# Turning the spectrum back on VectorE instead of TensorE in a long-convolution kernel

## The chip, the cores and the metric

The kernel runs on one core of a Trainium2 chip. The metric is the device time of one execution in microseconds (us). The core has five engines with queues of their own: TensorE (PE in the profile, its weight loads PEld), VectorE (DVE), ScalarE (ACT), GpSimd (POOL) and SyncE (SP), which here only issues DMAs. Each engine takes its instructions in the order in which the program lists them, and waits for the others through semaphores.

## The reference

One batch of 2048 tokens with 512 channels, all in float32. Two branches read the same layer norm, and their product is added to the input:

```python
xn = layernorm(x)                                   # (1, 2048, 512)
# branch A: state space convolution
P  = exp(dt*(A_re + 1j*A_im)[:, :, None] * l)       # (512, 128, 2048)
K  = einsum("dn,dnl,dn->dl", Cc, P, dt*Bc).real     # one kernel of 2048 taps for each channel
y  = irfft(rfft(xn, 4096) * rfft(K, 4096))[:2048] + xn * Dskip
# branch B: feed forward, 512 -> 1792 -> 512
g  = silu(gelu(xn @ w1 + b1) @ w2 + b2)
return x + y * g
```

## The kernel before, in words

The kernel has two parts. In the first, up to about 406 us, the feed-forward matrix products run on PE, while the other engines make the convolution kernels K and store them in HBM (`kgd`), with the order of all work written out by hand in the string `ORDER`. The gate `g` goes to HBM as `gd`, one array of 128 rows for each block of 128 channels. The change leaves the order of this part alone; only the places of the tokens in the tiles that `ln_load` and `ln_store` read and write, and so in `gd`, are others.

The second part is the convolution. It is a transform of 2048 points in two steps (32 x 64) on the signal and on the kernel, a product, and the way back in two steps. It takes the channels in four blocks `b` of 128 (`NB`), and each block in eight slots `g`. `slot(b, g)` issues the work of one slot; a loop calls it for all 32, and some lines behind the loop finish the last block. Three blocks overlap in it: block `b` is in the middle, block `b + 1` gets its first transform, and block `b - 1` its way back. The steps, by the names that the profile shows:

- `first_dft` (line 864, PE, tile `s` from `in` and `fc`; called F here): 32 products into four PSUM banks; `first_out` (870, ACT) copies the four to `X`.
- `second_dft` (883, PE, tile `s` from `X` and `mc`; S): 32 products of 64x64 weights into a tile `ri` of two banks. `spectrum` (891, ACT) copies the signal's half to `uh`, `product` (900, DVE) multiplies twice into `t`.
- `combine` (910 and 912, DVE): after two slots it makes the real and imaginary parts `Y`, in four instructions on 64 partitions each.
- `back_dft` (918, PE, tile `sa` from `tcn` and `Y`; B): 8 products of 128x128 in two banks for one `Y`; `back_out` (930, ACT) copies them to `Z`.
- `swing` (936, PE, tile `w`): 32 transposes of 128x128 for a block, in eight groups of four; `swing_out` (944, ACT) copies them to `bs`.
- `last_dft` (975, PE, tile `y` from `bs` and `gc`; L) twice for a block; `last_out` multiplies by the gate on DVE (982) and adds the input on POOL (983); `store` (992) writes the output with eight DMAs from SP.
- `tail_load` (961, 964) brings the gate and the input for it: 24 DMAs from SP for a block; `side_load`, `side_turn`, `kernel_load` and `side_skip` bring the signal and the kernel of block `b + 2`, with two POOL copies (839).

[...] Two tiles `ri` take four. The other four are given out in turn by `bank`, two with the tag `c` and two with the tag `a`; F takes all four at once, B two, L two, a swing one. A tile is given again when its last reader is done. In the slot, S comes first on PE, then the rest; B stands in the odd slots, for the `Y` that was combined two slots before, and F in the even ones:

```python
sa = (b, i - 1) if i else (b - 1, 3)
if sa[0] < 0 or g % 2 == 0:
    sa = None
```

Of the kernel before, what the change touches and what calls it, by code (L numbers as in the profile page):

```python
# [20 lines left out]
P = 128  # L21
# [109 lines left out]
def _shape_constants():  # L131
# [4 lines left out]
    cg = np.zeros((2, N1, 2, 3, N1))  # L136
    for hh in range(2):
        for c, v in enumerate((np.cos(a).T, -np.sin(a).T)):
            cg[hh, :, c, 0] = v
            cg[hh, :, c, 1:].reshape(N1, N1, 2)[:, :, hh] = v  # L140
    cg = cg.reshape(P, 3 * N1)
# [14 lines left out]
    ct = ct.reshape(P, N1, 2, 2, 2, 16).transpose(0, 1, 4, 5, 3, 2)  # L156
# [16 lines left out]
def kernel(  # L173
# [7 lines left out]
    x_t = u[0].rearrange("(n h j t a q) d -> t h a j n q d", n=N1, h=2, j=2, t=2, a=2)  # L181
    o_l = out[0].rearrange("(r j q) d -> j r q d", j=2, q=NQ)
    o_t = out[0].rearrange("(n h j t a q) d -> t h a j n q d", n=N1, h=2, j=2, t=2, a=2)
    x_l = u[0].rearrange("(r j q) d -> j r q d", j=2, q=NQ)
# [3 lines left out]
    xs_l = xs.rearrange("(r j q) d -> j r q d", j=2, q=NQ)  # L188
# [125 lines left out]
    def ln_load(n):  # L314
        if n == 2:
            ln["zi"] = wka.tile([P, TB, D], F32, tag="zi", name="x23")
        if n in (2, 3):
            x = ln["zi"][:, 2 * n - 4:2 * n - 2, :]
        else:
            x = wka.tile([P, 2, D], F32, tag="x", name=f"x{n}", bufs=2)  # L320
        for j in range(2):
            SY.dma_start(x[j * 64:(j + 1) * 64], x_l[j, :, 2 * n:2 * n + 2, :])
        ln[n] = x
# [31 lines left out]
    def ln_store(n):  # L355
        for j in range(2):
            SY.dma_start(xs_l[j, :, 2 * n:2 * n + 2, :], ln[n][j * 64:(j + 1) * 64])
# [430 lines left out]
    def open_mid():  # L788
# [3 lines left out]
        SB["gc"] = pm.tile([P, N1], F32, name="gc")  # L792
# [109 lines left out]
    def combine(b, j, c, eng, js=slice(0, 4)):  # L902
        t, w = sm[b, j]
        if (b, j) not in yy:
            yy[b, j] = SB["pm"].tile([P, 4, 2, P], F32, tag="Y", name=f"Y_{b}_{j}", bufs=2)
        Y = yy[b, j].rearrange("p j a (r x) -> p a r j x", r=2)
        for ka in range(2):
            r = slice(ka * 64, ka * 64 + 64)
            if c == 0:
                eng.tensor_sub(Y[0:64, ka, :, js], t[r, 0, :, js], w[r, 1, :, js])  # L910
            else:
                eng.tensor_add(Y[64:128, ka, :, js], t[r, 1, :, js], w[r, 0, :, js])

    def back_dft(b, j, h):
        Y = yy[b, j].rearrange("p j a m -> p (j a) m")
        p = bank(f"sa{b}_{j}_{h}")
        for e in range(4):
            PE.matmul(p[:, e, :], Y[:, 4 * h + e, :], SB["tcn"][:, 8 * j + 4 * h + e, :], start=True, stop=True)  # L918
        yy[b, j, h] = p

    def back_out(b, j, h, engs=(A,)):
        if (b, "Z") not in yy:
            yy[b, "Z"] = SB["pm"].tile([P, 32, 2, N1, 2], F32, tag="Z", name=f"Z{b}", bufs=2)
        k = 8 * j + 4 * h
        src = yy.pop((b, j, h)).rearrange("p k (x h c) -> p x h k c", h=2, c=2)
        dst = yy[b, "Z"][:, :, :, k:k + 4, :]
        w = 4 // len(engs)
        for i, eng in enumerate(engs):
            n = slice(w * i, w * i + w)
            eng.copy(dst[:, :, :, n], src[:, :, :, n]) if eng is A else eng.tensor_copy(dst[:, :, :, n], src[:, :, :, n])  # L930

    def swing(b, q4, jj, wide=None):
        Z = yy[b, "Z"].rearrange("p (j r t q) h k c -> p j r t q (h k c)", j=2, r=2, t=2)
        p = bank(f"w{b}_{q4}_{jj}") if wide is None else wide[:, jj]
        for e in range(4):
            PE.transpose(p[:, e, :], Z[:, jj, q4 // 2, q4 % 2, e, :], ident)  # L936
        yy[b, q4, jj] = p

    def swing_out(b, q4, jj, eng):
        if jj == 0:  # L940
            yy[b, q4, "s"] = SB["pm"].tile([P, 2, 4, P], F32, tag="bs", name=f"bs{b}_{q4}", bufs=3)
        dst = yy[b, q4, "s"][:, jj].rearrange("p e (x r) -> p e r x", r=2)
        src = yy.pop((b, q4, jj)).rearrange("p e (r x) -> p e r x", r=2)
        A.copy(dst, src) if eng is A else V.tensor_copy(dst, src)

    gx = {}
    gc2 = dsk.rearrange("p b d -> p (b d)")[:, :2 * N1]

    def tail_load(b, i, q=SY, rows=False):
        cs = slice(b * P, (b + 1) * P)  # L950
        t = gx.pop((b, i, "t"), None) or new_tail(b, i)
        gx[b, i] = t
        if rows:
            n = slice(4 * i, 4 * i + 4)
            q.dma_start(t[0], gd[b].rearrange("p (q m) -> p q m", m=P)[:, n])
            for j in range(2):
                q.dma_start(t[1][j * 64:(j + 1) * 64], x_l[j, :, n, cs])
            return
        for a in range(2):
            r = slice(a * 64, (a + 1) * 64)  # L960
            q.dma_start(t[0][r], gd[b].rearrange("(j n h) (t a q m) -> t h a j n q m", n=N1, h=2, t=2, a=2, m=P)[i // 2, i % 2, a])
            for j in range(2):
# [212 lines left out]
```

## Time and profile before

| | us |
|---|---|
| median of the runs (3) | 560.42 |
| lowest and highest run | 559.8, 560.91 |
| span of the profiled execution, first to last instruction | 558.0 |
| PE, DVE, ACT, POOL busy in it | 540.2, 454.2, 407.8, 296.3 |
| the four blocks of slots and the end, in the span | 405.89 to 558.0 |

The profiled execution's own time outside the profiler is not listed; its span is 2.42 us under the median, and that difference stands for what lies around the span. A line of the timeline gives the start, the length to the modelled end of the last instruction, the engine, the line, the tiles and the count; PE's float32 products appear as two records each, so B is x16, F, S x64. On PE, the distance from one start to the next is what a group takes, since the ends overlap.

### The profile page before, as it was taken

Reading aid. Unit: us, or ns where it says so; the run is one execution under the profiler, and the core shown is the slowest. Engines: PE = TensorE matmul, PEld = TensorE weight load, DVE = VectorE, ACT = ScalarE, POOL = GpSimd, SP = SyncE. Lnnn points to the kernel's source line nnn. Section 1 sums busy time; section 2 is a strip of 40 time slices with the busy share of each in tenths; the row PEclk is TensorE's granted clock in tenths of the full one; section 3 lists DMA queues with packets and bytes.
Section 4 is the critical chain, followed back from the end, with each engine's and each line's share of the span. In section 5 each row is a group of like instructions: output and inputs, shape, how many; then the busy total and the mean of one; then the engine's idle time right before and its main releaser. Section 6 shows DMA issues by size and latency. Waiting matters only on the chain.

```text
span 558.0 us, 17143 instructions
## 1 busy us (share of the span) xinstructions
PE 540.2 (97%) x7179; PEld 432.1 (77%) x7179; DVE 454.2 (81%) x697; ACT 407.8 (73%) x602; POOL 296.3 (53%) x403
## 2 busy tenths in 40 slices
PE   8899999999999999999999999999999999999995
PEld 7567777777777777767777777777889998988872
DVE  6899999999997799988988969877357657767874
ACT  3589997977598999668989798995355565564542
POOL 5639585776966769857718747540320305014323
PEclk9999999999999999999999999999999999999999
DMA  8959337267468392426167049205965583615945
GB/s 188 288 161 311 84 96 210 61 210 228 135 189 269 133 295 81 143 75 192 57 188 219 21 114 186 61 11 181 365 245 79 140 128 95 191 46 127 197 120 113
DMA packets 108345, 86.92 MB, mean 156 GB/s; under 512 B 44294, under 2 KB 87562, under 8 KB 108268
## 3 DMA queue, kind: packets, MB, share of 16 engines
q1 hardware_dynamic: 97584, 65.37, 43.8%
q0 software_dynamic: 9568, 19.93, 12.1%
q8 instruction: 56, 0.92, 0.7%
q10 hardware_dynamic: 1116, 0.53, 0.4%
q14 instruction: 21, 0.17, 0.1%
HBM read 52.25 MB, written 33.55 MB: 154 GB/s over the span
## 4 chain that ended last, share of the span: by engine, by line
PE 68%; DVE 16%; issue 6%; DMA 5%; SPq 2%; ACT 1%; POOL 1%; DVEq 0%; POOLq 0%
PE z L295 8%; PE z L296 7%; PE z L297 7%; PE f L256 7%; PE f L258 7%; PE f L257 7%; PE s L883 6%; PE kg L656 5%; PE s L864 4%; PE sa L918 3%; DMA w2s<-in_B_w_dram 2%; PE ph L595 2%; PE w L936 2%; DVE e L641 2%; DVE hl L282 2%
## 5 line engine op out<-in xcount | busy, mean ns | idle before, releaser
L618 POOL TENSOR_TENSOR mm<-mm,rc 128x32 f32<-128x32 f32 (+4 forms) x150 | 110.7, 738 | 11.8
L295 PE MATMUL z<-w2h,hh 128*128 128x512 f32 x224 | 97.9, 437 | 0.0
L256 PE MATMUL f<-xh,w1h 128*128 128x512 f32 x220 | 92.0, 418 | 0.5 <-ACT hf L270 0.5
L297 PE MATMUL z<-w2h,hl 128*128 128x512 f32 x224 | 88.5, 395 | 0.9 <-DVE hl L282 0.9
L296 PE MATMUL z<-w2l,hh 128*128 128x512 f32 x224 | 88.7, 396 | 0.0
L258 PE MATMUL f<-xh,w1l 128*128 128x512 f32 x220 | 86.9, 395 | 1.5 <-DVE w1l L241 1.5
L257 PE MATMUL f<-xl,w1h 128*128 128x512 f32 x220 | 86.7, 394 | 0.0
L883 PE MATMUL s<-X,mc 64*64 64x128 f32 x2048 | 63.5, 272 | 0.9 <-issue 0.9
L900 DVE TENSOR_TENSOR t<-s,uh 128x512 f32<-128x512 f32 x64 | 41.1, 685 | 25.9 <-ACT uh L891 25.6
L883 PEld LDWEIGHTS s<-X,mc 64*64 64x64 f32 x2048 | 56.0, 133 | 4.8 <-issue 2.7
L641 DVE TENSOR_TENSOR e<-mm,ra 128x1024 f32<-128x1024 f32 x32 | 47.8, 1495 | 4.7 <-POOL mm L618 3.2
L297 PEld LDWEIGHTS z<-w2h,hl 128*128 128x128 f32 x224 | 42.1, 188 | 11.7 <-DVE hl L282 1.8
L258 PEld LDWEIGHTS f<-xh,w1l 128*128 128x128 f32 x220 | 41.3, 188 | 11.9 <-DVE w1l L241 2.1
L615 POOL COPY mm<-rc 128x32 f32<-128x32 f32 x30 | 15.4, 512 | 65.4 <-DVE e L648 49.0
L256 PEld LDWEIGHTS f<-xh,w1h 128*128 128x128 f32 x220 | 41.5, 189 | 10.3 <-ACT hf L270 1.2
L282 DVE TENSOR_TENSOR hl<-hf,hh 128x512 fp32r<-128x512 f32 x56 | 46.7, 838 | 3.4 <-ACT hh L276 3.3
L295 PEld LDWEIGHTS z<-w2h,hh 128*128 128x128 f32 x224 | 42.5, 190 | 9.0
L609 DVE SCALAR_TENSOR_TENSOR ra<-ra,ph 128x512 f32<-128x512 f32 x64 | 43.6, 681 | 6.9 <-ACT ra L603 6.0
L296 PEld LDWEIGHTS z<-w2l,hh 128*128 128x128 f32 x224 | 42.3, 189 | 7.9
L257 PEld LDWEIGHTS f<-xl,w1h 128*128 128x128 f32 x220 | 41.4, 188 | 8.9
L870 ACT COPY X<-s 128x512 f32<-128x512 f32 x56 | 28.9, 598 | 25.6 <-PE s L864 25.6
L645 DVE TENSOR_TENSOR e<-mm,ra 128x1024 f32<-128x1024 f32 x32 | 45.6, 1425 | 0.0
(185 smaller groups left out, 1146.2 us busy)
## 6 DMA issues: line engine op xcount, KB each, us to landing
x<-in_A_u_dram SPq DMA_DIRECT2D x16, 256.0 KB
xs<-x SPq DMA_DIRECT2D x16, 256.0 KB
xt_h<-xh POOLq DMA_DIRECT2D x4, 1024.0 KB, 5.4
xt_l<-xl POOLq DMA_DIRECT2D x4, 1024.0 KB, 7.3
kgd<-ko SPq DMA_DIRECT2D x32, 128.0 KB
za<-zo SPq DMA_DIRECT2D x4, 1024.0 KB
xh<-xt_h POOLq DMA_DIRECT2D x4, 1024.0 KB, 6.8
xl<-xt_l POOLq DMA_DIRECT2D x4, 1024.0 KB, 10.1
```

Of the source, the lines that this page charges most:

```text
L256: PE.matmul(p, wh[:, k, :], xh[:, k, :], start=(k == 0), stop=False)
L257: PE.matmul(p, wh[:, k, :], xl[:, k, :], start=False, stop=False)
L258: PE.matmul(p, wl[:, k, :], xh[:, k, :], start=False, stop=(k == KD - 1))
L282: V.tensor_sub(hl, hf, hh)
L295: PE.matmul(z, hh[:, s], wh, start=(f0 == 0 and not rows), stop=False)
L296: PE.matmul(z, hh[:, s], wl, start=False, stop=False)
L297: PE.matmul(z, hl[:, s], wh, start=False, stop=(f0 == FA - 1))
L609: V.scalar_tensor_tensor(ra[:, 0, c], ra[:, 1, c], MAGIC, p, op0=ALU.subtract, op1=ALU.subtract)
L618: GP.tensor_mul(mv[:, :, 0:3:2, w:2 * w], mv[:, :, 0:3:2, 0:w], rc[:, 2 + 2 * i:4 + 2 * i, :].rearrange("p j c -> p c j").unsqueeze(3).to_ ...
L641: V.tensor_mul(e1, m1.unsqueeze(1).to_broadcast([P, 2, CH, N1]), ra[:, :, :, :N1])
L645: V.tensor_mul(e2[:, :, :, :H], m2[:, :, :H].unsqueeze(1).to_broadcast([P, 2, CH, H]), ra[:, :, :, dn])
L883: PE.matmul(p[ka * 64:(ka + 1) * 64, r, o, :, jj], mc[h, k, ((0, 2), (1, 0))[c][o], :], xf[b][h, c, :, k, :], start=(c == 0), stop=(c == 1 ...
```

## The change

The way back is laid out anew.

- The tables `ct`, `cg` and the choice of `k` in `second_dft` are ordered so that the two halves of 64 partitions of the products belong to different frequencies. `combine` works on 128 partitions: two instructions for one `Y` in place of four.
- `back_dft` sums over real and imaginary parts in PSUM: 16 products of 64x128 weights, two row halves side by side, each half into a bank of its own. It moves from the odd slots to the even ones: for the `Y` that the slot before combined.
- The transposes on PE, their copies and `bs` go. `turn` transposes `Z` on DVE in squares of 32x32: four instructions of 128x1024 for a block, in slots 5 and 6 of the block and in slots 1 and 2 of the next.
- `last_dft` is one step for a block, in slot 3: 32 products of 32x32 weights on 512 columns, into four banks. `last_gate` multiplies by the gate with four DVE instructions with a stride of two; `store` adds on POOL in slots 4 to 7, with four DMAs each.
- `first_dft` of the next block stands in slots 0, 1, 5 and 6, no more in 0, 2, 4 and 6, and behind `back_dft` where a slot has both.
- `tail_load` is five DMAs for a block (the gate in one of 1 MB), in slots 0 and 1; gate and input have one buffer each (`gb`, `xb`), for a whole block. For the last block they come on POOL's queue in slot 1.
- Tokens: position (n, c, q), of 32, 4 and 16, where there was (r, j, q), in `ln_load`, `ln_store` and all that follows.

```diff
-                            k, h = 4 * g + 2 * jj + ka, slice(r * 64, (r + 1) * 64)
+                            k, h = 8 * (g // 2) + 4 * ka + 2 * (g % 2) + jj, slice(r * 64, (r + 1) * 64)
...
+            yy[b, j] = SB["pm"].tile([P, 2, 4, P], F32, tag="Y", name=f"Y_{b}_{j}", bufs=2)
+        Y = yy[b, j][:, c].rearrange("p j (r x) -> p r j x", r=2)
+        if c == 0:
+            eng.tensor_sub(Y[:, :, js], t[:, 0, :, js], w[:, 1, :, js])
+        else:
+            eng.tensor_add(Y[:, :, js], t[:, 1, :, js], w[:, 0, :, js])
+
+    def back_dft(b, j, wide=None):
+        Y = yy.pop((b, j))
+        ps = [bank(f"sa{b}_{j}_{a}") for a in range(2)] if wide is None else [wide[:, a] for a in range(2)]
         for e in range(4):
+            for c in range(2):
+                for a in range(2):
+                    r = slice(64 * a, 64 * a + 64)
+                    PE.matmul(ps[a][:, e, :], Y[r, c, e, :], SB["tcn"][r, 8 * j + 2 * e + c, :],
+                              start=(c == 0), stop=(c == 1), skip_group_check=True)
+        yy[b, j, "p"] = ps
+
+    def back_out(b, j, engs=(A, A)):
+        if j % 2 == 0:
+            yy[b, "Z", j // 2] = SB["pm"].tile([P, N2, 2, N1 // 2], F32, tag="Z", name=f"Z{b}_{j // 2}", bufs=2)
+        for a, p in enumerate(yy.pop((b, j, "p"))):
+            k = 8 * (j % 2) + 4 * a
+            dst = yy[b, "Z", j // 2][:, :, :, k:k + 4]
+            src = p.rearrange("p k (c n) -> p n c k", c=2)
+            A.copy(dst, src) if engs[a] is A else engs[a].tensor_copy(dst, src)
+
+    def turn(b, h, i, n=2):
+        if i == 0:
+            yy[b, "T", h] = SB["pm"].tile([P, N2, N1], F32, tag="T", name=f"T{b}_{h}", bufs=2)
+        m = slice(i * N2 // n, (i + 1) * N2 // n)
+        V.transpose(yy[b, "T", h][:, m].rearrange("p n c -> p (n c)"), yy[b, "Z", h][:, m].rearrange("p n c k -> p (n c k)"))
...
+    def last_dft(b, hs=(0, 1), gs=range(G)):
+        if (b, "y") not in gx:
+            gx[b, "y"] = [bank(f"y{b}_{q}").rearrange("p e m -> p (e m)") for q in range(G)]
+        py = gx[b, "y"]
+        for h in hs:
+            T = yy[b, "T", h]
+            for g in gs:
+                for q in range(G):
+                    r = slice(q * N1, (q + 1) * N1)
+                    PE.matmul(py[q][g * N1:(g + 1) * N1], SB["gc"][r, h], T[r, 16 * g:16 * g + 16].rearrange("p n c -> p (n c)"),
+                              start=(h == 0), stop=(h == 1), skip_group_check=True)
...
+    ahead = {0: (0, 0), 1: (0, 1), 5: (1, 0), 6: (1, 1)}
 
     def slot(b, g):
...
+        if sa[0] < 0 or g % 2:
             sa = None
+        u = None if last else ahead.get(g)
         second_dft(b, g)
         if sa:
+            back_dft(*sa)
+        if u:
+            first_dft(b + 1, *u, range(G))
+        if b and g == 3:
+            last_dft(b - 1)
         spectrum(b, g)
         if sa:
+            back_out(*sa)
+        if u:
+            first_out(b + 1, *u)
         product(b, g)
+        if g % 2:
+            combine(b, i, 0, V)
             combine(b, i, 1, V)
+        if b and g in (1, 2):
+            turn(b - 1, 1, g - 1)
+        if g in (5, 6):
+            turn(b, 0, g - 5)
+        if b and g == 3:
+            last_gate(b - 1)
+        if b and 3 < g:
+            store(b - 1, g - 4)
...
+        wide = SB["ps"].tile([P, 2, 4, P], F32, tag="ri", name="wide", bufs=2)
+        back_dft(b, 3, wide)
+        last_dft(b, (0,))
+        back_out(b, 3, (A, V))
+        for i in range(2):
+            turn(b, 1, i)
+            last_dft(b, (1,), range(2 * i, 2 * i + 2))
+        last_gate(b)
+        for i, (eng, q) in enumerate(((V, SY), (V, A), (GP, SY), (GP, A))):
+            store(b, i, eng, q)
```

More of the change, by code (lines that the diff above doesn't have):

```diff
@@ L921, in back_out @@
[L921 to L944, printed above, removed]
+            yy[b, j] = SB["pm"].tile([P, 2, 4, P], F32, tag="Y", name=f"Y_{b}_{j}", bufs=2)
@@ L946, with tail_load @@
     gx = {}
[L947 to L949 removed]
+    def tail_load(b, q=SY, part=2, t=None):
         cs = slice(b * P, (b + 1) * P)
[L951 to L962, printed above, removed]
[L963 to L964 removed]
@@ L1029, in slot @@
         second_dft(b, g)
-        if b:
-            for q4 in ls.get(g, ()):
-                last_dft(b - 1, q4)
-                if not last:
-                    last_out(b - 1, q4, (GP, GP))
-                    store(b - 1, q4)
-        if nxt and g % 2 == 0:
-            first_dft(b + 1, i // 2, i % 2, range(G))
-        if sa:
-            back_dft(*sa, 0)
-            back_dft(*sa, 1)
+        if sa:
+            back_dft(*sa)
+        if u:
+            first_dft(b + 1, *u, range(G))
```

173 lines of the change are left out of this document (37 added, 136 removed).

## The prediction

> **What bounds the kernel now.** I read the page first, then the busy time of each engine in stretches cut where a block's first S starts, then the timelines of PE, ACT and DVE in the second block. The page's first line, and the stretches for blocks 0, 1, 2, 3 (up to the end of the last combine) and the end; columns are PE, PEld, DVE, ACT, POOL busy, PE's granted clock, the DMA share and GB/s.
>
> ```profile
> span 558.0 us, 17143 instructions
> ...
> 405.89:436.54 30.65, 29.80 (x817) 27.47 (x816) 19.31 (x30) 16.96 (x31) 7.10 (x8) 1.00 0.51 130
> 436.54:473.13 36.59, 36.59 (x897) 32.70 (x896) 23.55 (x36) 21.66 (x40) 7.92 (x8) 1.00 0.67 133
> 473.13:509.63 36.50, 36.50 (x898) 32.60 (x897) 24.76 (x36) 21.65 (x40) 5.91 (x7) 1.00 0.44 119
> 509.63:541.83 32.20, 30.43 (x651) 26.41 (x650) 28.03 (x45) 14.91 (x26) 14.19 (x22) 1.00 0.74 166
> 541.83:558.00 16.17, 9.21 (x68) 5.49 (x66) 7.30 (x11) 3.87 (x7) 5.03 (x4) 0.93 0.45 99
> ```
>
> Blocks 1 and 2 are PE alone: it is busy all of 36.59 and 36.50 us, with DVE at 24 and ACT at 22. Whatever leaves PE there is gained, as long as PE then waits for nothing. So the question is not only what PE has to do, but how long before each step its inputs and banks are ready. PE's timeline gives the price of each step, from one start to the next:
>
> ```profile
> 453.87 1.98 PE L883 MATMUL s<-X,mc 64*64 64x128 f32 x64
> 455.78 2.01 PE L864 MATMUL s<-fc,in 32*128 32x64 f32 x64
> 457.72 1.98 PE L883 MATMUL s<-X,mc 64*64 64x128 f32 x64
> 459.63 1.09 PE L975 MATMUL y<-bs,gc 64*32 64x512 f32 x16
> 460.65 2.05 PE L918 MATMUL sa<-tcn,Y 128*128 128x128 f32 x16
> 462.54 1.91 PE L936 MATMUL w<-ident,Z 128*128 128x128 f32 x16
> 464.38 1.98 PE L883 MATMUL s<-X,mc 64*64 64x128 f32 x64
> ...
> 478.89 2.05 PE L918 MATMUL sa<-tcn,Y 128*128 128x128 f32 x16
> 480.88 1.98 PE L883 MATMUL s<-X,mc 64*64 64x128 f32 x64
> ```
>
> S takes 1.91, F 1.94, half of L 1.02, B 1.89 to 1.99 (I take 1.98), sixteen transposes 1.84. A block has eight S, four F, four B, two halves of L and 32 transposes: 15.28 + 7.76 + 7.92 + 2.04 + 3.68 = 36.68, the stretch of 36.5 to 36.6. The chains beside it, on ACT and on DVE:
>
> ```profile
> 455.96 0.59 ACT L891 COPY uh<-s 128x512 f32<-128x512 f32 x1 [1.03 <-issue]
> 457.81 2.05 ACT L870 COPY X<-s 128x512 f32<-128x512 f32 x4 [1.26 <-PE s L864]
> ...
> 462.74 0.59 ACT L930 COPY Z<-sa 128x512 f32<-128x512 f32 x1 [0.31 <-PE sa L918]
> ```
>
> ```profile
> 452.25 1.39 DVE L912 TENSOR_TENSOR Y<-t,t 64x512 f32<-64x512 f32 x2
> 453.65 1.40 DVE L910 TENSOR_TENSOR Y<-t,t 64x512 f32<-64x512 f32 x2
> 456.58 1.29 DVE L900 TENSOR_TENSOR t<-s,uh 128x512 f32<-128x512 f32 x2 [1.53 <-ACT uh L891]
> 460.81 1.35 DVE L982 TENSOR_TENSOR gb<-y,gb 128x512 f32<-128x512 f32 x2 [2.94 <-PE y L975]
> ```
>
> From the end of S (455.78) to its `uh` 0.18, from the end of F (457.72) to `X` 0.09, from B (462.54) to `Z` 0.20, from `uh` to the product 0.03. A copy takes 0.59 alone, 0.51 in a row of four; a product pair 1.29, a combine instruction 0.70, a gate instruction 0.68. And PE waits in order:
>
> ```profile
> 509.63 3.72 PE L883 MATMUL s<-X,mc 64*64 64x128 f32 x128
> 514.17 0.46 PE L918 MATMUL sa<-tcn,Y 128*128 128x128 f32 x2 [0.82 <-DVE Y L910]
> ```
>
> ```profile
> 511.12 2.21 DVE L912 TENSOR_TENSOR Y<-t,t 64x512 f32<-64x512 f32 x2
> 513.34 1.40 DVE L910 TENSOR_TENSOR Y<-t,t 64x512 f32<-64x512 f32 x2
> ```
>
> This is the one place where B came close to its `Y`: PE stood still, and went on 0.14 after the first of the two L910 (513.34 + 0.69). From any DVE or ACT release I count 0.10 to 0.14.
>
> **The change, part by part.** *Removed from PE:* the transposes, 3.68 in each of blocks 1, 2 and 3 and in the end. *L:* twice the 16 records of a half in a grid twice as fine; 2.04 if sixteen small tiles run at twice the rate of eight, 4.1 if not. Up to some 3 us it only shortens a wait below, so it costs nothing; at 4.1 about 1 us a block. *B:* as many column passes as before, two at a time; S, with the same passes in four small tiles, takes 1.91, so 1.98 stays, and 1.91 is the lower end. *Removed from ACT:* eight copies to `bs`; ACT was not the bound. *DVE:* combine halves, 16 times 0.70 becomes 8 times, 5.6 less; four turns are added. The trace has no DVE transpose. The nearest rows are a two-input DVE operation of the same 128x1024 at its fastest (from the chain), and a POOL copy of 128x1024 (from the groups):
>
> ```profile
> 206.52 1.13 DVE e L645
> ```
>
> ```profile
> L839 POOL COPY in<-raw 128x1024 f32<-128x1024 f32 x4 | 7.9, 1996 | 26.6 <-PE s L864 22.1 <-issue 4.4
> ```
>
> I take 1.13, the engine's own row; 2.00 is the upper end. At 1.13 DVE's block stays near 23 us. [...]
>
> *What is late next.* Four new waits come from the order in the slot.
>
> (1) B for a `Y` of the slot before. From the end of that slot's S: 0.18 + 0.59 + 0.03 + 1.29 + 0.03 + 1.40 + 0.12 = 3.64 until PE may read both halves of `Y`. If PE has only the next S in between (1.91), it waits 1.73; four of B's 32 records need only the first half, so 1.48. F or L in the odd slot covers it. Uncovered are slot 4 of block 0, slots 2 and 6 of block 3 (no F there), and slot 0 after every block.
>
> (2) F right behind B, in slots 0 and 6. F needs four banks with its first four products, B holds two: 0.20 + 0.51 + 0.59 + 0.10 = 1.40 of standing until both `Z` copies are out. Before, an S lay between.
>
> (3) F of slot 1 behind F of slot 0, and the first S of a block behind F of slot 6: the four `X` copies take 0.09 + 2.05 + 0.10 = 2.24, and one S of 1.91 lies between: 0.33.
>
> (4) L takes all four banks, and B of slot 4 needs two of them. The gates stand on DVE behind product and combine of slot 3: from the end of that S 0.18 + 0.59 + 0.03 + 1.29 + 0.03 + 1.40 + 2 x 0.68 + 0.12 = 5.00, less L and S of 3.95: 1.05.
>
> In a block's slot 0, (3) has held S by 0.33 while `uh` before it comes 0.1 later behind the copies, so (1) is 1.25 there.
>
> *The sum.* Block 0: no transposes to lose; slot 1 0.33, slot 4 1.48, slot 6 1.40: +3.2. Blocks 1 and 2: -3.68, and 0.33 + 1.25 + 1.40 in slot 0, 0.33 in slot 1, 1.05 in slot 4, 1.40 in slot 6, together 5.76: +2.1 each. Block 3 has no F: eight S, four B, L are 25.24; 0.33 + 1.25, 1.48, 1.05, 1.48 of waits are 5.59; then 3.52 from the last S to the last `Y`: 34.35 against 32.20, +2.15. POOL's four adds now follow the gates, and in the row at 511.12 combine beside POOL's adds took 2.21 for 1.39; once where nothing covers it: +0.8.
>
> The end, old rows first:
>
> ```profile
> 540.96 0.87 DVE L910 TENSOR_TENSOR Y<-t,t 64x256 f32<-64x256 f32 x2
> ...
> 545.74 1.29 DVE L944 COPY bs<-w 128x512 f32<-128x512 f32 x2 [0.74 <-PE w L936]
> ```
>
> ```profile
> 548.93 2.51 POOL L983 TENSOR_TENSOR last<-last 128x512 f32<-128x512 f32 x2 [1.92 <-DVE last L982]
> ```
>
> ```profile
> 550.23 2.76 SPq L992 DMA_DIRECT2D out_dram<-last  x6
> ```
>
> ```profile
> 551.47 0.88 ACTq L992 DMA_DIRECT2D out_dram<-last  x2
> 552.46 2.13 ACTq L1014 DMA_DIRECT2D out_dram<-last  x3
> ```
>
> The last `Y` was complete at 541.83, the last issue over at 554.59, and 3.4 later the span ends. New, from the last `Y`: B 1.85 after it, the copy on DVE 0.20 + 0.65, two turns 1.13 + 1.13, the last quarter of L 0.51 + 0.12: 5.6; four gates, since each store needs all four: 8.5. DVE's adds 9.2 and 9.9, POOL's (1.26 each) 9.8 and 11.0; four issues of 0.46 for each store, two stores on each queue: SP until 12.9, ACT until 13.5; with 3.4, 16.9 against 16.17: +0.7.
>
> *Costed at nothing.* Loads in the new token order have the same bytes in pieces of the same length, and the first part has no other work. SP issues 19 DMAs a block fewer; but the gate's 1 MB waits for the add of slot 7, which on POOL stands behind the two copies of `side_turn` (2.00 each), and behind it on SP stand the input's loads. The gate is first read in slot 3, some 20 us into the block, the input in slot 4: that slack hides it; without it each microsecond late counts. Behind SP's waits stand `side_load` and `kernel_load`, needed a block later.
>
> Together 3.2 + 2.1 + 2.1 + 2.15 + 0.8 + 0.7 = 11.05: a span of 569.1. The median of the runs is 2.4 above the span, so 571.5.
>
> **The rivals.** *Faster: PE passes its waits.* If PE's queue brings the next ready step forward (the S behind a waiting B, the B behind a waiting F), only the work counts: block 0 as before, blocks 1 and 2 -3.7 each, block 3 28.8 for 32.2, the end +0.7: 550 at best, 552 if DVE holds some of it. It decides where the waits of a middle block sum to less than 3.7. Against it: at 514.17 the rows are in program order and PE idles. *No change: the banks are free.* Without (2), (3) and (4), as if copies and gates came out in time, 1.40 x 5, 0.33 x 6 and 1.05 x 3 go, while (1) grows by 0.23 three times: 11.4 less, 560.1. Against: B's and L's tiles end whole, not one by one. *Smaller: `Y` is in time.* Without (1), three times 1.25 and 1.48, 8.2 less: 563.3. Against: the 3.64 is five rows in series. *Larger: weights show.* B's weight loads, from the groups:
>
> ```profile
> L918 PEld LDWEIGHTS sa<-tcn,Y 128*128 128x128 f32 x256 | 30.0, 191 | 8.3 <-issue 3.4 <-ACT uh L891 3.4 <-PE s L883 1.0
> ```
>
> If those of 64-row tiles were not hidden, 32 of 0.191 with two tiles at once make B 3.06, and fifteen of them add 16: 587. F, with weights as wide and 64 records in 1.94, speaks against.
>
> *Larger: the clock.* In the end stretch PE is busy 9.21 of 16.17 and was granted 0.93; in blocks at 95% and more, 1.00. With 5.8 of 38.8 idle PE would be busy 85% in a middle block. The end stretch lost 0.07 of 16.17 by the clock, 1.1; if each of the 14 waits over a microsecond lost as much, 15 would be added: 587. [...] The longest idle here is 1.5, and nothing in the trace of before shows it for waits that short.
>
> **How the numbers follow.** The forecast 0.68, with 562 to 578 for it: down to less overlap of waits and B at 1.91, up to turns at 2.00 (+3.2, mostly in block 3 and the end) and L at 4.1 (+3). Passing 0.09, banks free 0.05, `Y` in time 0.07, weights 0.06, clock 0.05. The range 560 to 582 leaves out passing, weights and clock, 0.20. A change under 0.2% could not be told here. Faster 0.09, the same 0.03 (half of the bank case), slower 0.88.
>
> **What would show it.** No `w` and `bs` rows; Y twice in place of four times. PE idle of about 1.5 ahead of `sa` in slot 4 of block 0, released by DVE `Y`; of 1.4 ahead of F in slots 0 and 6, released by ACT `Z`; of 1.0 ahead of `sa` in slot 4, released by the gates. Blocks of about 34, 38.7, 38.7 and 35. Wrong, if PE's busy share in blocks 1 and 2 is near all again, or if `turn` is over 2 us.

## The result, and the profile after

The changed kernel takes 700.19 us (median of 4 runs, 697.2 to 703.35) against 560.61 us (559.8 to 560.91) for the kernel before in the same runs: a ratio of 1.2493, 95% interval 1.2454 to 1.2531. Slower was forecast, but at 571.5 us. The profiled execution has a span of 701.6 us, 143.6 over the 558.0 before.

The page's first lines, and the slices of PE, its granted clock and the DMA rate:

```profile
span 701.6 us, 17483 instructions
...
PE 557.4 (79%) x7439; PEld 443.5 (63%) x7439; DVE 443.4 (63%) x675; ACT 390.8 (56%) x571; POOL 287.8 (41%) x390
...
PE   5242519389298959999999999999998979899772
```

PE is busy 557 us, much as before (540), in a span 144 us longer: the work hardly grew, the waiting did, and it stands at the left end, in the first part, which the prediction had set aside (the first S starts at 522.37, before at 405.89). The first 100 us, the kernel before ahead (columns as in the prediction):

```profile
0.00:100.00 100.00, 93.66 (x677) 73.50 (x678) 88.70 (x188) 76.50 (x119) 63.42 (x114) 1.00 0.68 187
```

```profile
0.00:100.00 100.00, 34.55 (x146) 28.19 (x146) 26.38 (x72) 14.84 (x25) 13.60 (x48) 0.68 0.24 77
```

PE does little more than a third of its work there, at a granted clock of 0.68, and the DMA engines move 77 GB/s for 187: an idle PE beside idle DMA engines. The loads come through SP's queue. Its timeline before, then after (start, us of issue, engine, line):

```profile
0.75 2.48 SPq L322 DMA_DIRECT2D x<-in_A_u_dram  x4
3.28 0.59 SPq L222 DMA_DIRECT2D w1s<-in_B_w_dram  x1
3.91 0.50 SPq L227 DMA_DIRECT2D w2s<-in_B_w_dram  x1
...
15.19 3.02 SPq L357 DMA_DIRECT2D xs<-x  x4
```

```profile
0.75 5.55 SPq L316 DMA_DIRECT2D x<-in_A_u_dram  x4
6.34 4.97 SPq L216 DMA_DIRECT2D w1s<-in_B_w_dram  x1
11.35 5.49 SPq L221 DMA_DIRECT2D w2s<-in_B_w_dram  x1
...
40.82 15.62 SPq L351 DMA_DIRECT2D xs<-x  x4
```

The same four loads and four stores of 256 KB, but the issue of one weight load behind them now takes 4.97 and 5.49 us where it took 0.59 and 0.50, and a stage that was stored at 15.19 is stored at 40.82. The rate, in 40 slices of the first 25 us (before, 111 to 439 from the fourth slice on):

```profile
GB/s 0 0 2 14 7 20 46 39 43 46 46 49 52 52 52 52 52 52 52 107 318 60 46 52 52 52 52 46 151 308 35 45 47 46 52 52 52 52 52 48
```

The plateau at 52 GB/s is the thing to see: it is not noise from a crowded path but a fixed rate. The diff has one change that could set it: `ln_load` and `ln_store` moved from 64 rows in one outer dimension to `x_l[2 * j:2 * j + 2, :, ...]`, an outer dimension of 2 over 32 rows each, on the DRAM side.

### The profile page after: what moved, and what is told of

It is laid out like the page before. It is cut to its first block, busy times and chain, and to the rows that moved or that the text cites. A ratio compares the mean times of both kernels' runs of the same rounds, so it can differ in the third digit from the quotient of the medians.

```text
span 701.6 us, 17483 instructions
## 1 busy us (share of the span) xinstructions
PE 557.4 (79%) x7439; PEld 443.5 (63%) x7439; DVE 443.4 (63%) x675; ACT 390.8 (56%) x571; POOL 287.8 (41%) x390
## 4 chain that ended last, share of the span: by engine, by line
PE 50%; DMA 17%; DVE 12%; SPq 9%; issue 6%; ACT 3%; POOL 2%; POOLq 0%; DVEq 0%; ACTq 0%
DMA lh<-pcd 8%; PE s L877 6%; PE f L250 5%; PE z L289 5%; PE f L251 5%; PE f L252 5%; PE z L290 5%; PE z L291 5%; DMA w2s<-in_B_w_dram 4%; PE sa L913 4%; PE kg L650 4%; PE s L858 3%; SPq L216 3%; DMA in<-kgd 3%; SPq L351 2%
## 5 line engine op out<-in xcount | busy, mean ns | idle before, releaser
L250 PE MATMUL f<-xh,w1h 128*128 128x512 f32 x220 | 95.1, 432 | 31.6 <-ACT hf L264 16.2
L612 POOL TENSOR_TENSOR mm<-mm,rc 128x32 f32<-128x32 f32 (+4 forms) x150 | 114.5, 763 | 11.9
L251 PE MATMUL f<-xl,w1h 128*128 128x512 f32 x220 | 89.5, 407 | 0.0
L252 PE MATMUL f<-xh,w1l 128*128 128x512 f32 x220 | 89.3, 406 | 0.0
L877 PE MATMUL s<-X,mc 64*64 64x128 f32 x2048 | 68.3, 282 | 10.3 <-issue 7.6
L877 PEld LDWEIGHTS s<-X,mc 64*64 64x64 f32 x2048 | 59.8, 139 | 17.2 <-issue 11.6
L609 POOL COPY mm<-rc 128x32 f32<-128x32 f32 x30 | 13.1, 435 | 111.5 <-DMA rc<-recd 59.5
L589 PE MATMUL ph<-cbs,lh 96*128 96x512 bf16 x64 | 25.6, 400 | 40.1 <-DMA lh<-pcd 36.0
L635 DVE TENSOR_TENSOR e<-mm,ra 128x1024 f32<-128x1024 f32 x32 | 45.9, 1433 | 9.4 <-POOL mm L612 6.4
L264 ACT ACTIVATE hf<-f,b1s 128x512 f32<-128x512 f32 x56 | 38.5, 689 | 15.6 <-PE f L252 10.5
```

What stands on the lines that cost most here:

```text
L250: PE.matmul(p, wh[:, k, :], xh[:, k, :], start=(k == 0), stop=False)
L251: PE.matmul(p, wh[:, k, :], xl[:, k, :], start=False, stop=False)
L252: PE.matmul(p, wl[:, k, :], xh[:, k, :], start=False, stop=(k == KD - 1))
L612: GP.tensor_mul(mv[:, :, 0:3:2, w:2 * w], mv[:, :, 0:3:2, 0:w], rc[:, 2 + 2 * i:4 + 2 * i, :].rearrange("p j c -> p c j").unsqueeze(3).to_ ...
L635: V.tensor_mul(e1, m1.unsqueeze(1).to_broadcast([P, 2, CH, N1]), ra[:, :, :, :N1])
L877: PE.matmul(p[ka * 64:(ka + 1) * 64, r, o, :, jj], mc[h, k, ((0, 2), (1, 0))[c][o], :], xf[b][h, c, :, k, :], start=(c == 0), stop=(c == 1 ...
```

## The experiments

Theory A: a DMA is shared out over as many DMA engines as its outermost dimension allows, so these loads and stores run on two of sixteen, and everything behind them on SP's queue waits. Theory B: the second part's new order lost the time and the first part only shows a late start. By A the outer dimension alone decides. A time with a ratio to the kernel before in brackets is the median of four runs; the others are of one run, beside 560.3 for the kernel before. All edits but the second are to the changed kernel, and from the fourth on its loads and stores of the layer norm are four DMAs.

**Four DMAs of 32 rows.**

```
-        for j in range(2):
-            SY.dma_start(x[j * 64:(j + 1) * 64], x_l[2 * j:2 * j + 2, :, 2 * n:2 * n + 2, :])
+        for c in range(G):
+            SY.dma_start(x[c * N1:(c + 1) * N1], x_l[c, :, 2 * n:2 * n + 2, :])
```

and the same in `ln_store`.

> The changed kernel, with the loads and stores of the layer norm in four DMAs of 32 rows each in place of two of 2 x 32 rows; the same bytes to the same places. Theory A (a DMA is shared out over the DMA engines by its outermost dimension, and that is 2 in the changed kernel): the first S of block 0 stands at 406 to 410 us again, as before the change (405.9), in place of 522.4; the second part still takes 175 to 180 in place of 152; about 585 to 590 in all. Rival B (the new places of the tokens in HBM are slow to read and write in any shape): the first part stays at about 520 and the whole at about 700.

586.13 us (1.0475, 1.0446 to 1.0504). **The kernel before, with the new order's loads alone** (`x_n` is its input seen as `(n c q) d -> c n q d`; the same in `ln_store`, nothing else):

```
-            SY.dma_start(x[j * 64:(j + 1) * 64], x_l[j, :, 2 * n:2 * n + 2, :])
+            SY.dma_start(x[j * 64:(j + 1) * 64], x_n[2 * j:2 * j + 2, :, 2 * n:2 * n + 2, :])
```

> The kernel before, with only the layer norm's loads and stores in the new token order and in two DMAs of 2 x 32 rows each; the way back is the old one, so gate and convolution meet at wrong tokens. If these transfers alone make the first part slow (theory A or rival B): the first S at 515 to 525 us, 670 to 680 in all. If the first part's loss comes from something else in the change (tables, placement in SBUF): 406 and about 561.

673.2 us, against 560.27. **One DMA with an outer dimension of 4**:

```
-        for j in range(2):
-            SY.dma_start(x[j * 64:(j + 1) * 64], x_l[2 * j:2 * j + 2, :, 2 * n:2 * n + 2, :])
+        SY.dma_start(x, x_l[:, :, 2 * n:2 * n + 2, :])
```

> The changed kernel, with each load and store of the layer norm in one DMA of 4 x 32 rows: fewer DMAs, outermost dimension 4. Theory A: twice as many DMA engines as with 2, so these transfers run at about twice the rate (near 100 GB/s where 50 is seen in the first 60 us), and half or more of the 116 us goes: first S at 440 to 470, 620 to 650 in all. Rival B: no better than the changed kernel, 522 and 700. If instead the count of DMAs mattered, half as many would bring some of it back without a change of the rate.

621.16 us. The rates of the three in the first 25 us, in the order told:

```profile
GB/s 0 0 42 263 269 256 223 262 210 207 211 307 280 33 169 241 356 254 216 202 232 256 282 236 243 203 223 252 331 420 348 203 151 216 169 215 291 316 365 317
```

```profile
GB/s 0 0 2 14 26 13 52 43 39 33 29 39 46 46 46 46 52 52 52 57 180 267 33 52 52 52 46 52 102 206 197 44 44 46 52 52 52 46 52 52
```

```profile
GB/s 0 0 3 26 0 13 46 217 266 84 92 95 164 324 57 83 81 79 105 105 105 105 105 105 88 79 80 31 110 320 280 257 195 162 141 37 26 52 111 262
```

Outermost 2: 52 GB/s, in either kernel. Outermost 4: 105. Outermost 32: no plateau, mostly 200 to 400. So 26 GB/s for each unit of that dimension where it is 2 or 4, and A holds for them. The places of the tokens in HBM are the same in all three, so they are not what is slow: the form of these 16 loads and 16 stores is worth 701.6 - 582.5 = 119 us of the 143.6, and costs the kernel before 113 when it is put in alone. The share of the 16 DMA engines agrees: on the plateau of the changed kernel (7.50 to 11.20) it is 0.13, where two of sixteen are 0.125; at 4 the slices at 105 GB/s show two tenths, where four of sixteen are 0.25; with 32 rows most slices show eight or nine tenths. Which engines carry a DMA is not shown.

**What is left.** With four DMAs the first S starts at 406.17, as before (405.89), and the second part takes 176.3 us for 152.1, +24.2 where the prediction had +11.05. Its stretches for blocks 1 and 3 and the end, cut as in the prediction:

```profile
440.25:485.25 45.00, 39.48 (x964) 34.20 (x960) 22.31 (x32) 17.16 (x33) 8.10 (x8) 0.92 0.56 113
...
524.60:562.90 38.30, 29.15 (x744) 24.43 (x736) 24.86 (x36) 9.61 (x18) 8.14 (x9) 0.98 0.62 136
562.90:582.50 19.60, 6.78 (x95) 3.20 (x92) 8.00 (x10) 0.58 (x1) 3.43 (x2) 0.69 0.25 54
```

Block 0 (34.08, forecast 33.85) and block 2 (39.35, 38.6) are near the forecast; block 1 (45.00, 38.7), block 3 (38.30, 35.15) and the end (19.60, 16.9) are not. PE's waits in these 176 us, by what ended them (total, times, longest):

```profile
PE s L877 <- issue: 6.9, 3, 3.8
PE sa L913 <- DVE Y L902: 5.3, 4, 2.0
PE wide L913 <- DVE Y L902: 2.9, 1, 2.9
PE y L954 <- issue: 1.5, 1, 1.5
PE s L858 <- ACT Z L924: 1.5, 5, 0.3
```

The lines with DVE and ACT are the forecast waits. The "issue" ones, waits that nothing in this view ended, are not: PE stops in the middle of a step whose inputs and banks are there. One of them, and what follows:

```profile
453.01 1.63 PE L877 MATMUL s<-X,mc 64*64 64x128 f32 x49
...
458.41 1.13 PE L877 MATMUL s<-X,mc 64*64 64x128 f32 x15 [3.77 <-issue]
459.47 3.78 PE L913 MATMUL sa<-tcn,Y 64*128 64x128 f32 x32
```

S halts after 49 of its 64 records, for 3.77 us, and the next B takes 3.78 us for 2.06: PE at half clock behind the halt (granted 0.50 from 458 to 462). Two theories: the transfers stop PE, or its own order does (waits, banks, the idle clock).

**By the order.** F ahead of B in slots 0 and 6:

```
-        if sa:
-            back_dft(*sa)
         if u:
             first_dft(b + 1, *u, range(G))
+        if sa:
+            back_dft(*sa)
```

> e1 with the first DFT ahead of the back DFT in slots 0 and 6 (and its copies ahead of the other's), nothing else. By the waits of the prediction: in slot 0 the waits for Y (1.25) and for the banks of the back DFT (1.40) become one of 1.2 for two X copies, in slot 6 1.4 becomes 1.2; about 5 us less in three blocks, 580 to 582. If PE's waits do not come from the order of these two (PE takes what is ready, or another resource holds it): no change, 586.

580.24 us (1.0358, 1.0339 to 1.0378), as expected. The waits (1) and (2) of the prediction are real, and their going is worth 5.9 here; the halt stayed (4.11 us). The old places instead (B in odd slots, F in 0, 2, 4, 6, L in two halves of two banks):

```
-    ahead = {0: (0, 0), 1: (0, 1), 5: (1, 0), 6: (1, 1)}
+    ahead = {0: (0, 0), 2: (0, 1), 4: (1, 0), 6: (1, 1)}
-        if sa[0] < 0 or g % 2:
+        if sa[0] < 0 or g % 2 == 0:
+        ls = ({4: (0, 1), 5: (2, 3)} if last else {5: (0, 1), 7: (2, 3)}).get(g) if b else None
```

> The kernel with rows of 32 (e1), and in the slots the order of before: back DFT in the odd slots for the Y of two slots before, first DFT in slots 0, 2, 4, 6, the last DFT in two halves of two banks (slots 5 and 7, in the last block 4 and 5), turns in slots 7, 0, 2, 3; all new arithmetic stays. If the waits that the new slot order makes are what the second part lost (forecast of the prediction): blocks 1 and 2 are PE's work alone, 15.3 + 7.8 + 8.2 + 2.3 = 33.5 each (45.0 and 39.4 in e1, 36.6 before), block 0 about 30.7, block 3 about 30; 550 to 556 in all, faster than before. If the new arithmetic itself (64-row products, 32x32 tiles, turns) or traffic is what costs: little better than e1, 575 or more.

577.85 us (1.0321, 1.0285 to 1.0357): missed. The waits for `Y` and banks went, but for the last `Y`, and halts of 3.00, 3.17, 1.77 and 1.41 us came or stayed. The order alone does not decide them. The one of 3.00 is of another kind: it stands in block 0, ahead of every load of gate and input, and S goes on (417.93) when DVE's products, which had waited 5.63 for the DMA of `gd`, come out. PE kept busy with transposes of the identity while it waits for the last `Y` and ahead of the last quarters of L:

```
+        for e in range(28):
+            PE.transpose(wide[:, e % 2, e % 4], ident, ident)
         back_dft(b, 3, wide)
...
+        for e in range(36):
+            PE.transpose(idle[:, e % 2, e % 4], ident, ident)
```

> e1 with 28 transposes of the identity on PE while it waits for the last Y, and 36 more while it waits for the last turns; their results are overwritten or not used. Theory (the granted clock falls in PE's idle stretches of 2 to 3 us, and the next step pays for it): the last back DFT takes 2.1 in place of 3.3 us, the last quarters of L 1.0 in place of 1.7, the end is 1.5 to 2.5 us shorter: 583.5 to 585. Rival (the slow records come from something else): no change or up to 1 us more.

584.1 us (1.0420, 1.0392 to 1.0449). The slow steps in the end are thereby shown as an effect of idling in this kernel (the end was granted 0.69 without the transposes): with them B takes 2.10 for 3.36, a half of L 1.14 for 1.68. It buys little, since copies, turns and gates on ACT and DVE hold the end.

**By moving the transfers.** The signal's pieces over slots 2 to 5, POOL's loads of the last block in slot 3:

```
-        if last and g == 1:
+        if last and g == 3:
...
-        if b + 2 < NB and g == 3:
-            side_load(b + 2)
+        if b + 2 < NB and 2 <= g < 6:
+            side_piece(b + 2, g - 2)
```

> e1 with the signal's load of the block after next (four DMAs in pieces of 64 bytes) spread over slots 2 to 5 in place of all in slot 3, and the last block's loads on POOL's queue in slot 3 in place of 1. Theory: the 3.8 us in block 1 and the 2.4 us in block 3 that PE stands in the middle of a step, with nothing that the profile names, are PE's next instructions coming late behind this traffic, and what follows at half the granted clock (2 us more) comes of that; both shrink to under 1 us, the whole to 577 to 581. Rival: those stops are a property of the new program and its slot order; they stay, 585 to 587.

585.08 us (1.0446, 1.0401 to 1.0490): missed, halts of 2.95 and 3.25 stayed. The loads of gate and input in 256 KB pieces over four to seven slots:

```
-        if b and g < 2:
-            tail_load(b - 1, SY, g)
+        if b:
+            tail_load(b - 1, SY, *{0: ((0, 1), ()), 1: ((2,), (0,)), 2: ((3,), (1,)), 3: ((), (2, 3))}.get(g, ((), ())))
```

> e1 with the loads of gate and input for the way back in pieces of 256 KB, one or two in a slot (slots 0 to 3; for the last block one in each of slots 1 to 7 on POOL's queue) in place of 2 MB at once; bytes and places are the same. Theory: PE's stops in the middle of a step (3.8 us in block 1, 2.4 and 1.5 in block 3 of e1) are its next instructions waiting behind those 2 MB in the DMA engines; with small pieces they go below 1 us each and half the clock losses behind them too: 576 to 580, against 586. Rival (spreading the signal's load moved nothing, so traffic is not it): stops as in e1, 585 to 588.

585.16 us (1.0456, 1.0409 to 1.0504): missed, one halt is 5.14. Old places, paced loads and transposes in one:

> e4 (rows of 32, the old slot order) with the paced loads of e8 and the transposes of e6. If slot order, instruction supply and clock are all that the second part lost: block 0 about 31, blocks 1 and 2 about 35 (two halves of L at 1.9 each in place of one step of 2.3), block 3 about 32, the end 17: 557 to 562, no slower than before. If the paced loads do not stop the stops: 572 to 577.

585.19 us (1.0431, 1.0380 to 1.0481): missed; halts stayed, and in block 3 B waited 5.32 for gates whose pieces came late. Moving transfers did not tell whether they are the cause; leaving them out does.

**By leaving transfers out** (a memset on POOL fills each tile).

```
         side[b] = t
+        if b > 1:
+            GP.memset(t, 0.0)
+            return
```

> Changed kernel with the layer norm's loads and stores in four DMAs of 32 rows, and the loads of the signal for blocks 2 and 3 (2 MB in 64-byte runs, in blocks 0 and 1) left out: a memset on POOL fills their tile instead, so blocks 2 and 3 compute on zeros. If the stops of TensorE in the middle of a step (3.77 us in block 1) come from these transfers, block 1 goes from 45.0 us to 38.5 to 40, block 0 and block 3 stay near 34 and 38, and the run comes to 577 to 580 us. If the stops come from the order of TensorE's own work, block 1 stays at 44 to 46 and the run at 584 to 587.

590.02 us: the signal's loads are not the cause, halts of up to 3.3 stayed.

```
-            q.dma_start(g.rearrange("p q m -> p (q m)"), gd[b])
+            GP.memset(g, 0.0)
...
-            for c in range(G):
-                q.dma_start(x[c * N1:(c + 1) * N1], x_l[c, :, :, cs])
+            GP.memset(x, 0.0)
```

> As the four-DMA form of the changed kernel, with the loads of gate and input on the way back left out in every block (memsets on POOL fill their tiles). If the stops in block 3 (2.40 and 1.52 us, with the steps at half the granted clock behind them) come from those transfers, block 3 goes from 38.3 us to 34.5 to 35.5, block 2 stays near 39.3 and block 1, which keeps the signal's loads, near 43 to 45: 580 to 583 us. If the stops come from the order of TensorE's own work, block 3 stays at 37.5 to 39 and the run at 584 to 587.

574.57 us, less than expected, since the halt in block 1 went too. Both left out:

> Both sets of loads left out, memsets in their place, so the second part is left with its stores of the output alone. If transfers stop TensorE, no stop over 1 us is left in blocks 1 to 3, these take 38.3 to 39.5, 38.3 to 39.5 and 34.5 to 35.5 us (the forecast waits alone), and the run comes to 572 to 576 us. If TensorE's own order stops it, the run stays at 584 to 587.

574.13 us, hardly less. So at these places it is the loads of gate and input. PE's waits without them (the kernel that keeps the signal's loads):

```profile
PE sa L913 <- DVE Y L902: 6.1, 5, 2.0
...
PE s L877 <- issue: 0.4, 2, 0.2
```

8.4 us of "issue" have become 0.4; the forecast waits remain. Which load, and what about it?

> The four-DMA form of the changed kernel, with the loads of the gate on the way back left out (1 MB per block, one DMA of 8 KB runs; a memset on POOL fills the tile) and those of the input kept. If the gate's long runs stop TensorE, the stops go as they went without both loads: block 1 at 38 to 39 us, block 3 at 34.5 to 35.5, the run at 574 to 577 us. If the input's 512-byte runs stop it, the stops of 3.8 us in block 1 and 2.4 in block 3 stay: 582 to 587 us.

> The same with the loads of the input left out (1 MB per block in 512-byte runs) and those of the gate kept. If the input's loads stop TensorE: 574 to 577 us. If the gate's do: 582 to 587 us. If it is the sum of both that fills the DMA engines, this run and the one without the gate both lose most of their stops and come to 574 to 579 us.

576.42 without the gate's, 576.35 without the input's: either removal takes most of the loss away (longest halt 2.1 and 1.3), so it takes both loads together. Then the sizes of the kernel before (8 DMAs of 128 KB and 16 of 64 KB for 1 of 1 MB and 4 of 256 KB), same bytes, same slots:

```
+        for i in range(4):
+            n = slice(4 * i, 4 * i + 4)
...
+                    q.dma_start(g[r, n], gd[b].rearrange("p (q m) -> p q m", m=P)[r, n])
...
+                    q.dma_start(x[c * N1:(c + 1) * N1, n], x_l[c, :, n, cs])
```

> The four-DMA form of the changed kernel, with the gate and input of the way back loaded in the sizes of the kernel before: 8 DMAs of 128 KB and 16 of 64 KB per block, 2 KB and 512-byte runs, in the same slots as now. If the size of a DMA is what stops TensorE, the stops go: 574 to 578 us. If only the bytes in flight count, they stay: 582 to 587 us.

574.34 us: the halts go away (0.7 at most) although all the bytes are moved. SP's timeline in block 1 shows what differs, first large, then small:

```profile
443.39 0.37 SPq L940 DMA_DIRECT2D gb<-gd  x1
443.81 4.57 SPq L943 DMA_DIRECT2D xb<-in_A_u_dram  x4
453.22 8.62 SPq L813 DMA_DIRECT2D raw<-xs  x4
```

```profile
444.43 4.99 SPq L944 DMA_DIRECT2D gb<-gd  x8
449.49 10.89 SPq L947 DMA_DIRECT2D xb<-in_A_u_dram  x16
460.48 6.33 SPq L813 DMA_DIRECT2D raw<-xs  x4
```

The 2 MB are handed over in 5 us, or trickle out over 16 (SP takes 4.99 us to issue the 8 and 10.89 for the 16), and the signal's loads start 7 us later. The stretches around the halt, of the kernel with large and of that with small loads (the last columns are clock, DMA share, GB/s):

```profile
450.00:454.00 4.00, 3.91 (x124) 3.43 (x120) 2.11 (x4) 2.09 (x5) 0.00 (x0) 1.00 1.23 191
454.00:458.00 4.00, 0.64 (x22) 0.50 (x14) 1.62 (x2) 1.15 (x3) 0.00 (x0) 0.98 0.96 115
458.00:462.00 4.00, 3.59 (x39) 3.26 (x40) 1.75 (x3) 0.58 (x1) 0.00 (x0) 0.50 1.06 134
```

```profile
451.00:455.00 4.00, 4.00 (x136) 3.76 (x130) 1.04 (x2) 2.64 (x5) 0.00 (x0) 1.00 0.70 170
455.00:459.00 4.00, 4.00 (x105) 3.71 (x101) 3.81 (x6) 2.64 (x5) 0.00 (x0) 1.00 0.39 107
```

With large loads the DMA share is 1.00 from 446 to 450, 1.23 to 454 and nine tenths or more in each slice to about 456.6; with small ones it is 1.05 from 447 to 451 and then 0.70 and 0.39. The DMA share within the halt, 454.64 to 458.41, in 40 slices, and a row of the DMA queues in it:

```profile
DMA  9999999999999999999975432211111111111125
...
q8 instruction: 1, 0.02, 2.1%
```

The page lists this queue, q8, with 58 packets and 0.95 MB. My guess was that it brings PE's instructions, and that they come late through a full path. No view names what a packet carries; the packets' own times in the trace agree with the guess. Each packet has 16384 bytes; 0.95 MB over PE's 14963 records, weight loads counted, is about 64 bytes a record, so by this estimate a packet stands for some 256. In the kernel with large loads the halts in the middle of a step end 2048, 1792, 1793 and 256 records apart: PE stops where such a block ends. It goes on 1.3 to 1.6 us after the end of a q8 packet (the one in this halt runs from 455.55 to 456.80, PE goes on at 458.41), and in no profiled run with the four DMAs of 32 rows, nor in the kernel before, does it pass such a place in the second part sooner than 1.2 us behind its packet. What differs is when the packet moves: 5.1 us after PE has passed the end of the block before (450.47), behind the 2 MB; with small loads 1.7 us after it, without those loads 0.4. The run without the signal's loads fits: its halt of 2.49 us ends at 461.73, when the DMA engines are nearly idle (a share of 0.18 from 458 to 462), but its packet had moved 4.1 us late, from 459.09 to 460.34. How packets take turns on the DMA engines is not shown, nor why 256 KB pieces over more slots did not help (the packet ahead of the halt of 5.14 moved 6.3 us late).

**Both ends together.** The old places without those loads, and then the two orders with all loads mended:

> The form with the last transforms at the places of the kernel before (577.85 us) without the loads of gate and input on the way back: what the change would take if nothing stopped TensorE. Its stops of 3.00, 3.17, 1.41, 1.77 us and the steps at half the granted clock behind them go, the two halves of L at 1.95 us for 1.14 stay: 560 to 566 us. At 572 or over, the stops are not the loads'.

563.28 us, as expected, and still 3 over the 560.32 of before. But this is not yet the kernel that nothing stops: of the four halts two stayed, 2.65 in block 0, behind the DMA of `gd`, and 1.06 in block 2, at the end of a block of 256 records, and PE's "issue" waits come to 4.9 us, for 0.9 before. What the change would take without them is not shown.

> Both loads mended (the layer norm's in four DMAs of 32 rows, gate and input in 128 KB and 64 KB pieces) and the steps of the way back at the places of the kernel before. Without those loads this order took 563.28 us. If the small pieces free TensorE's supply as they did at the changed kernel's own places (586.13 to 574.34), it takes 562 to 566 us, 0.3 to 1.0% over the kernel before; if their crowding with other transfers brings stops back, 568 to 577 us.

> The changed kernel's places with both loads mended and F ahead of B in slots 0 and 6. The wait for Y (2.0 us in slot 0) and the four waits for banks (0.30) go, as they did without the small loads (586.13 to 580.24), and no stop was left to move them into: 567.5 to 570.5 us against 574.34.

571.35 us (1.0193, 1.0147 to 1.0238) and 571.89 (1.0177, 1.0132 to 1.0222): both over what was expected. At the old places halts of 2.75 and 1.41 stayed, much as without those loads. The small loads of block 2's input also came late for the gates in block 3, and B behind them waited 4.11:

```profile
538.51 1.29 DVE L969 TENSOR_TENSOR gb<-y,gb 128x512 f32<-128x512 f32 x2 [7.08 <-DMA xb<-in_A_u_dram]
```

With F first, the swap brings 2.5 (from 574.34) where it brought 5.9 beside the halts: waits of 0.47 and 0.66 are left ahead of B, and some of these B run at half clock (last section). No form tried reaches the kernel before.

## Why the prediction was wrong, and where it was right

The step that failed is the first sentence under *Costed at nothing*: "Loads in the new token order have the same bytes in pieces of the same length, and the first part has no other work." Bytes and pieces are indeed the same. I did not look at the third property of a DMA, its outermost dimension, which went from 64 to 2 on the DRAM side, although the diff showed it, and I let the first part out of every rival. It cost 119 us, over ten times all that I had summed. What could have warned me stood in the profile of before: SP's queue, which brings these rows, brings the weights behind them, and PE is busy 93.66 of the first 100 us on both.

The second such step: "SP issues 19 DMAs a block fewer", noted as harmless. Fewer and larger DMAs handed 2 MB over within 5 us, and the q8 packet that PE went on behind moved 5.1 us after the end of the block before, for 1.7 with small loads; 582.5 - 572.6 = 9.9 us went there (11.8 from the median 586.13 to the one run of 574.34).

With both mended, the changed kernel's second part can be read against the sum (span 572.6, 14.6 over before; forecast 11.05). Its stretches from one slot-0 B to the next, and then from the last B to the end:

```profile
445.79:484.55 38.76, 35.91 (x961) 31.29 (x961) 23.50 (x33) 17.15 (x32) 9.31 (x8) 1.00 0.62 130
484.55:522.11 37.56, 35.91 (x960) 31.28 (x961) 22.38 (x33) 17.15 (x32) 7.72 (x11) 1.00 0.51 134
522.11:552.18 30.07, 25.17 (x640) 21.18 (x641) 22.16 (x33) 8.40 (x15) 15.78 (x24) 1.00 0.70 156
552.18:572.60 20.42, 7.07 (x96) 4.00 (x96) 8.36 (x10) 0.58 (x1) 3.43 (x2) 0.76 0.24 52
```

- Blocks 1 and 2: 76.32 us from B to B for the two, forecast 77.3 for two blocks. PE is not busy all of them any more: 35.91 of 37.6 to 38.8. Right, if a little high.
- The waits, in this kernel's rows:

```profile
426.23 2.43 PE L913 MATMUL sa<-tcn,Y 64*128 64x128 f32 x32 [1.05 <-DVE Y L902]
...
448.10 0.44 PE L858 MATMUL s<-fc,in 32*128 32x64 f32 x4
448.84 2.48 PE L858 MATMUL s<-fc,in 32*128 32x64 f32 x60 [0.30 <-ACT Z L924]
451.25 1.98 PE L877 MATMUL s<-X,mc 64*64 64x128 f32 x64
453.16 2.09 PE L858 MATMUL s<-fc,in 32*128 32x64 f32 x64
...
460.98 2.35 PE L958 MATMUL y<-T,gc 32*32 32x512 f32 x64
...
465.17 2.54 PE L913 MATMUL sa<-tcn,Y 64*128 64x128 f32 x32
...
484.55 2.34 PE L913 MATMUL sa<-tcn,Y 64*128 64x128 f32 x32 [2.03 <-DVE Y L902]
```

  (1) In slot 4 of block 0 B stands 1.05 and then takes 0.38 longer than its 1.98 (428.59 to the next S): 1.43, forecast 1.48. In slot 0 it stands 0.91, 2.03 and 0.89 in blocks 1, 2 and 3 and takes 0.3 longer, forecast 1.25; for the 2.03 see POOL's adds below. (2) F behind B in slot 0 goes from 448.10 to 451.25, 3.15 for 1.94: 1.21, forecast 1.40; four of F's records go first, which I had not counted. (3) F of slot 1 starts 1.91 after its S and takes 2.02 for 1.94: 0.1, forecast 0.33. (4) B behind the gates runs 0.48 longer than 2.06, and nothing else: forecast 1.05.
- L, bounded between 2.04 and 4.1: 2.28 from start to start (463.26). It stays near the lower bound. At the old places its halves, with eight tiles at a time, took 1.88 each: splitting L costs 1.5 more a block.
- The turn at 1.13, upper end 2.00: 1.22 to 1.24 alone and 2.37 for two, so the fast end.
- The end, 16.9 from the last `Y`: here 572.6 - 552.64 = 20.0. Three terms are mis-sized. The last B ends 3.35 after the last `Y`, forecast 1.85 (it takes 3.81: half clock behind a wait of 2.89). The copy on DVE, which I put beside that on ACT, came after it, 0.5 more; the profile names ACT's copy as what it waited for, and the profile of before had the same wait (at 543.25, 1.43 for ACT's copy to `Z`). DVE's two adds, beside POOL's, take 2.36 for the 1.4 of the sum.

```profile
556.66 0.69 DVE L924 COPY Z<-wide 128x512 f32<-128x512 f32 x1 [4.03 <-ACT Z L924]
557.39 2.37 DVE L930 STREAM_TRANSPOSE T<-Z 128x1024 f32<-128x1024 f32 x2
```

- POOL's adds beside combine, +0.8: the term is real, but came a block earlier. In slot 0 of block 2 a combine instruction took 1.84 (at 482.56) where it takes 0.69, beside POOL's add, and B waited 2.03 for 0.9. In block 3 combine takes 0.68 to 0.78 an instruction; from its first S (1.90 after 517.24) to the last `Y` (552.64) it takes 33.5, forecast 35.15 with that term.
- The rivals: PE passes no wait and the banks are not free early. The clock, at 0.05, came in part: not at every wait, but behind single ones (block 0 was granted 0.91 in this run and took 2.7 longer to the first slot-0 B than in the run with large loads) and in the end (0.76, 0.93 before). These two are more than the 3.5 us that the span stands over the sum. Steps at half clock stood behind waits of 0.47 to 2.9 us, and not behind every such wait. Halts of PE beside large transfers (3.77 us in block 1) were on no list.

The sign of the forecast thus rested on a mechanism that holds: with both loads mended the kernel is at 574.34, in the range of 560 to 582 and 2.8 over the 571.5. That close it is partly by luck: the way to the first B of block 1 came out 2.4 over and the end 3.1, the rest 2.1 under. The time around the span, 2.4 in the sum, is 1.8 (703.35 for a span of 701.6). The prediction was of that kernel and not of the one in the diff.

## What to carry to other kernels

When a layout changes, read each DMA's access pattern from the outside in: here bytes and run length stayed the same while the outermost dimension fell from 64 to 2, and the rate from slices of 111 to 439 GB/s to 52. A flat plateau in the row of GB/s, with PE (busy 34.55 of the first 100 us) and the DMA engines (a share of 0.24) both idle, is what that looked like. Merging small loads is a change of its own: here it moved the burst, and PE stood for 3.77 us in the middle of a step whose inputs were there. Such a halt that nothing in the list of waits explains is worth a look at the packets of the queue "instruction".

## What the runs showed of the hardware that was not expected

- In the loads and stores of the layer norm, 26 GB/s for each unit of the outermost dimension: 52 at 2, 105 at 4.
- PE halted at the end of a block of some 256 of its records until 1.2 to 1.7 us after a q8 packet of 16384 bytes had moved: halts of up to 5.14 us. The one of 3.77 stood in a burst of 2 MB, handed over within 5 us, with a DMA share of 0.96 to 1.23; with the same bytes at the same places in DMAs of 64 and 128 KB 0.7 at most was left. Halts of this kind up to 0.55 us stand in the kernel before too (412.98).
- A step ran at half clock behind a wait of 0.47 us, and another behind the same wait did not. Two B of slot 6, in blocks 0 and 1, in the kernel with F first and small loads (granted clock 0.62 and 1.00):

```profile
437.15 3.91 PE L913 MATMUL sa<-tcn,Y 64*128 64x128 f32 x32 [0.47 <-ACT X L864]
...
476.38 2.54 PE L913 MATMUL sa<-tcn,Y 64*128 64x128 f32 x32 [0.47 <-ACT X L864]
```

  What decides between the two was not found.
